# Merging two split weight loads and splitting the load of x in a one-token attention and MLP block

## The chip, the cores and the metric

The kernel runs on one core of a Trainium2 chip. The metric is the device time of one execution in microseconds (us). Most executions of this kernel agree within 0.3%. A profiled execution has a span somewhat shorter than its time: 136.3 us of 138.12 us for the kernel before. Positions below ("at 82 us") are counted from the start of the profiled span.

## The reference

One decoding step for a batch of 4. Attention with 32 query heads and 4 key/value heads over the last 2048 positions is followed by a gated MLP. Each part has a layernorm ahead of it and a residual around it. All data are bfloat16.

```python
h  = x + attention(layernorm(x), k_cache, v_cache, wq, wo)     # wq 1024x4096, wo 4096x1024
hn = layernorm(h)
h2 = h + (silu(hn @ w1) * (hn @ w3)) @ w2                      # w1, w3 1024x3584, w2 3584x1024
```

Each weight is read once: 8 MiB each of wq, K, V and wo, and 7 MiB each of w1, w3 and w2. That is 55.6 MB for four rows of activations, so the question is whether the load stream ever stops.

## The kernel before

All large loads share one ring of 160 KiB in each of the 128 partitions. The sync engine's queue issues them in a fixed plan, each as soon as the bytes that it overwrites have been read.

```python
    plan = [
        ("wq", load_rows, (0, wq_v, N_Q, 0, 4)),            # runs of 32 KiB per partition
        ("wq", load_rows, (32 * KIB, wq_v, N_Q, 4, 4)),
        ("k", load_kv, (64 * KIB, A_k_cache, 0)),
        ("k", load_kv, (96 * KIB, A_k_cache, 2)),
        ("v", load_kv, (128 * KIB, A_v_cache, 0)),
        ("v", load_kv, (0, A_v_cache, 2)),
        ("wo", load_rows, (32 * KIB, wo_v, D, 0, 32)),      # 64 KiB
        ("w1", load_rows, (96 * KIB, w1_v, N_F, 0, 8)),     # 56 KiB
        ("w3", load_rows, (0, w3_v, N_F, 0, 4)),            # 28 KiB
        ("w3", load_rows, (28 * KIB, w3_v, N_F, 4, 4)),
        ("w2", load_rows, (56 * KIB, w2_v, D, 0, 17)),
        # ... cut: three smaller pieces of w2
    ]
    # ... cut
    x_sb = act.tile([B, D], BF16)
    nc.scalar.dma_start(out=x_sb[:], in_=x_flat)
    load_next(5)
    # ... cut: layernorm of x_sb, transposed to xnT; x is loaded again, spread, as x_q
    for kc in range(KC):                                    # 8 rows of wq in each partition
        # ... cut: 8 matmuls q_ps <- xnT[kc], wq row kc
        if kc == RQ - 1:
            load_next()                                     # second half of v, over wq's first rows
    # ... cut: K transposes, scores, softmax, output product OT
    for i in range(IO):
        # ... cut: 4 matmuls y_ps <- o4, wo row i
        if i == 11:
            load_next()
    load_next()
    # ... cut: residual, second layernorm -> hnT
    gate_up("w1", g_ps)
    # ... cut: eg, gs: the silu of g_ps
    gate_up("w3", u_ps)
    nc.vector.tensor_tensor(out=hg[:], in0=u_ps[:, :, :HF], in1=gs[:], op=ALU.mult)
    # ... cut: hg transposed to hgT, then 112 matmuls y2_ps <- hgT, w2 rows
```

## Time and profile before

Before the prediction there were three runs, with a median of 138.23 us (138.06 to 138.29).

| reading | value | view |
|---|---|---|
| share of the load queue in the span of 16 DMA engines | 95.3% | page, queues |
| first and last packet of that queue | 1.74 us, 132.67 us | the trace's packet records |
| bytes over that stretch | 55.58 MB in 130.9 us, 424 GB/s | the same |
| normalised second row (hnT) ready, w1 there | 92.3 us, 99.1 us | timeline |
| hgT ready, first piece of w2 there | 122.0 us, 126.3 us | timeline |

The packet records hold the start, duration and size of every packet of every DMA queue. Grouped by size, the packets of the load queue have nearly constant durations: 84 ns for 2 KiB, 611 for 16, 1062 for 28, 1213 for 32, 2116 for 56 and 2418 for 64 KiB. A straight line through them is 8.7 ns + 0.0368 ns per byte.

First the page of the kernel before: the DMA engines' busy tenths in 40 slices of the span, the load queue (packets, MB, share of 16 engines) and the chain that ended last.

```profile
DMA  5999899999999999997988989989799999989960
...
q1 hardware_dynamic: 2592, 55.58, 95.3%
...
DMA 58%; PE 21%; ACT 13%; DVE 5%; issue 1%; SPq 0%; ACTq 0%
```

The DMA row is at 8 or 9 tenths nearly everywhere after the first slice. In its middle the chain runs through TensorE and ScalarE work, which is not a contradiction. Loads were queued ahead of that work, so the stream went on while the chain followed the computation.

Next, the waits of the kernel before: who waited, for whom, us in total, times, the longest.

```profile
PE q_ps L215 <- DMA ring<-in_A_wq_dram: 12.0, 2, 6.1
...
PE g_ps L403 <- DMA ring<-in_B_w_dram: 9.0, 1, 9.0
PE u_ps L403 <- DMA ring<-in_B_w_dram: 8.3, 2, 5.3
PE y_ps L433 <- DMA ring<-in_B_w_dram: 8.3, 3, 7.1
...
PE y_ps L353 <- DMA ring<-in_A_wo_dram: 2.0, 1, 2.0
```

TensorE waits for every weight in turn, so it has time to spare in each stage that reads a weight. The timeline of the kernel before (start, duration, engine, line, what, idle before it):

```profile
13.05 3.58 PE L215 MATMUL q_ps<-ring,xnT 128*4 128x512 bf16 x32 [6.05 <-DMA ring<-in_A_wq_dram]
...
22.55 3.15 PE L215 MATMUL q_ps<-ring,xnT 128*4 128x512 bf16 x32 [5.92 <-DMA ring<-in_A_wq_dram]
...
107.50 3.13 PE L403 MATMUL u_ps<-ring,hnT 128*32 128x448 bf16 x32 [3.00 <-DMA ring<-in_B_w_dram]
...
115.98 3.17 PE L403 MATMUL u_ps<-ring,hnT 128*32 128x448 bf16 x32 [5.34 <-DMA ring<-in_B_w_dram]
...
120.33 1.70 DVE L425 STREAM_TRANSPOSE hgT<-hg 128x896 bf16<-128x896 bf16 x1
...
126.30 3.82 PE L433 MATMUL y_ps<-ring,hgT 128*32 128x256 bf16 x68 [7.14 <-DMA ring<-in_B_w_dram]
```

Half of the q and u matmuls run while the other half of their weight is still on its way. hgT is ready 4.3 us before w2's first piece.

### The profile page before, as it was taken

The page shows a single profiled execution, that of the slowest core. Times are in us where ns is not written, and L with a number is a line of the kernel's source. Part 1 is how long each engine was busy: PE and PEld are TensorE (multiplying, and loading weights), DVE is VectorE, ACT ScalarE, POOL GpSimd, SP SyncE. Part 2 cuts the span into 40 slices and gives each one's busy share as a digit, 9 for nine tenths or more (in the row PEclk, how much of TensorE's full clock was granted, in tenths as well). Part 3 has the DMA queues.
Part 4 walks back from the last instruction along what each step waited for, and adds up shares of the span by engine and source line. Part 5 has one row for each costly group of instructions (what it writes and reads, how often), then busy time and mean ns, then how long its engine had stood idle before and what let it go on. Part 6 is the DMA issues. An engine that isn't in the chain of part 4 may idle for free.

```text
span 136.3 us, 2302 instructions
## 1 busy us (share of the span) xinstructions
PE 67.9 (50%) x1035; PEld 42.9 (31%) x1035; DVE 42.6 (31%) x73; ACT 31.0 (23%) x36; POOL 1.7 (1%) x8
## 2 busy tenths in 40 slices
PE   0101803698989889105259538830096440900960
PEld 0100201274656565001149427610043210300840
DVE  6440000244444444609940030160000695070000
ACT  0400000155555646092944000000003300000001
POOL 5000000000000000000000000000000000000000
PEclk9999999999999999965555865897557777555577
DMA  5999899999999999997988989989799999989960
GB/s 156 462 462 443 385 413 418 423 447 423 428 437 409 437 437 423 435 582 341 538 385 365 524 365 442 459 353 522 328 412 463 434 437 447 429 388 409 426 261 5
DMA packets 2662, 55.75 MB, mean 409 GB/s; under 512 B 312, under 2 KB 344, under 8 KB 604
## 3 DMA queue, kind: packets, MB, share of 16 engines
q1 hardware_dynamic: 2592, 55.58, 95.3%
q8 instruction: 8, 0.13, 0.3%
q10 hardware_dynamic: 60, 0.02, 0.1%
q14 instruction: 2, 0.02, 0.0%
HBM read 55.59 MB, written 0.01 MB: 408 GB/s over the span
## 4 chain that ended last, share of the span: by engine, by line
DMA 58%; PE 21%; ACT 13%; DVE 5%; issue 1%; SPq 0%; ACTq 0%
DMA ring<-in_B_w_dram 42%; DMA ring<-in_A_wq_dram 16%; PE kt_ps L263 9%; ACT kT L269 6%; PE scores_ps L248 5%; ACT z L304 3%; PE q_ps L215 2%; PE g_ps L403 2%; DVE rmax L280 2%; ACT Pm L285 2%; PE OT_ps L326 2%; DVE pT L294 1%; DVE z L300 1%; ACT L285 1%; DVE q_sb L225 1%
## 5 line engine op out<-in xcount | busy, mean ns | idle before, releaser
L269 ACT COPY kT<-kt_ps 128x1024 bf16<-128x1024 bf16 x16 | 15.8, 1014 | 12.0 <-PE kt_ps L263 12.0
L263 PE MATMUL kt_ps<-ident,ring 128*128 128x128 bf16 x256 | 16.4, 219 | 0.0
L263 PEld LDWEIGHTS <-ring 128*128 128x128 bf16 x256 | 14.3, 98 | 5.0 <-issue 4.9
L267 DVE COPY kT<-kt_ps 128x1024 bf16<-128x1024 bf16 x16 | 11.1, 691 | 15.2 <-PE kt_ps L263 15.2
L215 PE MATMUL q_ps<-ring,xnT 128*4 128x512 bf16 x64 | 6.7, 596 | 12.0 <-DMA ring<-in_A_wq_dram 12.0
L403 PEld LDWEIGHTS <-hnT 128*32 128x32 bf16 x128 | 5.3, 137 | 23.1 <-issue 20.5
L248 PE MATMUL scores_ps<-kT,qz 128*32 128x512 bf16 x64 | 9.9, 609 | 3.1 <-ACT kT L269 3.1
L326 PE MATMUL OT_ps<-z,ring 128*128 128x32 bf16 x256 | 7.4, 185 | 6.7 <-ACT z L304 5.0
L403 PE MATMUL u_ps<-ring,hnT 128*32 128x448 bf16 x64 | 6.3, 572 | 8.3 <-DMA ring<-in_B_w_dram 8.3
L403 PE MATMUL g_ps<-ring,hnT 128*32 128x448 bf16 x64 | 5.4, 525 | 9.0 <-DMA ring<-in_B_w_dram 9.0
L433 PE MATMUL y_ps<-ring,hgT 128*32 128x256 bf16 x112 | 5.7, 370 | 8.4 <-DMA ring<-in_B_w_dram 8.3
L326 PEld LDWEIGHTS <-ring 128*128 128x128 bf16 x256 | 7.3, 103 | 7.4 <-issue 7.4
L433 PEld LDWEIGHTS <-hgT 128*32 128x32 bf16 x112 | 4.4, 129 | 10.3 <-issue 6.1
L215 PEld LDWEIGHTS <-xnT 128*4 128x4 bf16 x64 | 2.1, 116 | 16.2 <-issue 15.9
L353 PE MATMUL y_ps<-ring,o 128*32 128x256 bf16 x128 | 5.8, 365 | 2.0 <-DMA ring<-in_A_wo_dram 2.0
L443 ACT CAST res<-y_ps 128x256 bf16<-128x256 f32 x1 | 0.4, 372 | 26.5 <-PE y_ps L433 26.5
L304 ACT ACTIVATE z<-pt_ps,mask 128x512 bf16<-128x512 f32 x8 | 5.3, 687 | 3.5 <-DVE z L300 3.5
L225 DVE TENSOR_SCALAR q_sb<-q_ps 128x512 bf16<-128x512 f32 x1 | 0.7, 690 | 17.2 <-PE q_ps L215 17.2
L353 PEld LDWEIGHTS <-o 128*32 128x32 bf16 x128 | 4.8, 130 | 3.8 <-issue 3.1
L300 DVE TENSOR_SCALAR z<-pt_ps,mask 128x512 bf16<-128x512 f32 x8 | 5.5, 740 | 1.2 <-ACT z L304 0.8
L296 PE MATMUL pt_ps<-pT,perm 128*128 128x512 bf16 x4 | 2.4, 607 | 6.8 <-DVE pT L294 6.8
L417 DVE RECIPROCAL eg<-eg 128x896 f32<-128x896 f32 x1 | 5.8, 5753 | 0.0
(73 smaller groups left out, 40.5 us busy)
## 6 DMA issues: line engine op xcount, KB each, us to landing
ring<-in_A_wq_dram SPq DMA_DIRECT2D x2, 4096.0 KB, 16.8
ring<-in_A_k_cache_dram SPq DMA_DIRECT2D x4, 2048.0 KB, 25.5
ring<-in_A_v_cache_dram SPq DMA_DIRECT2D x4, 2048.0 KB, 40.2
ring<-in_B_w_dram SPq DMA_DIRECT2D x1, 7168.0 KB
ring<-in_B_w_dram SPq DMA_DIRECT2D x2, 3584.0 KB, 28.6
ring<-in_B_w_dram SPq DMA_DIRECT2D x1, 4352.0 KB
ring<-in_B_w_dram SPq DMA_DIRECT2D x1, 1792.0 KB
ring<-in_B_w_dram SPq DMA_DIRECT2D x1, 768.0 KB
```

The lines of the kernel that those rows point to most:

```text
L215: nc.tensor.matmul(q_ps[QD * g : QD * g + B, hf * 512 : (hf + 1) * 512], lhsT=xnT[:, kc, :], rhs=wq_t[:, c0 : c0 + 512], start=(kc == 0), ...
L248: nc.tensor.matmul(scores_ps[QD * g : QD * (g + 1), n * 512 : (n + 1) * 512], lhsT=qz[:, b, g * QD : (g + 1) * QD], rhs=kT_v[:, g, :, :], ...
L263: nc.tensor.transpose(out=kt_ps[:, jj, :], in_=k_v[:, n * NJ + t * TB + jj, :], identity=ident[:])
L267: nc.vector.tensor_copy(out=kT[:, t * TB : (t + 1) * TB, :], in_=kt_ps[:])
L269: nc.scalar.copy(out=kT[:, t * TB : (t + 1) * TB, :], in_=kt_ps[:])
L300: nc.vector.tensor_scalar(out=z[:, :, g, :], in0=pt_ps[:], scalar1=mask[:, g : g + 1], scalar2=None, op0=ALU.mult)
L304: nc.scalar.mul(out=z[:, :, g, :], in_=pt_ps[:], mul=mask[:, g : g + 1])
L326: nc.tensor.matmul(OT_ps[:, b, :], lhsT=loaded["v"][b][:, j, :], rhs=PTz[j // NJ][:, (j % NJ) * B + b, :, :], start=(j == 0), stop=(j == J ...
L353: nc.tensor.matmul(y_ps[QD * j : QD * (j + 1), :], lhsT=o4[:, i, :, :].rearrange("p b s -> p (b s)"), rhs=loaded["wo"][i][:, j * CG : (j + ...
L403: nc.tensor.matmul(out_ps[QD * j : QD * (j + 1), hf, :HF], lhsT=hnT[:, k, :], rhs=loaded[kind][k][:, c0 : c0 + HF], start=(k == 0), stop=( ...
L417: nc.vector.reciprocal(out=eg[:], in_=eg[:])
L433: nc.tensor.matmul(y2_ps[QD * j : QD * (j + 1), :], lhsT=hgT[:, i, :], rhs=loaded["w2"][i][:, j * CG : (j + 1) * CG], start=False, stop=(i ...
```

## The change

The intent is larger DMA packets and fewer loads. wq becomes one load with runs of 64 KiB and w3 one load with runs of 56 KiB. w3 can then be issued only after wo's twelfth row has been read, because it lies over wo's first twelve rows. The second half of v, which lies over wq's first rows, is now issued after all q matmuls instead of after half of them. x is loaded in three column pieces. The loads share eight semaphores in turn, so the split of x also shifts which earlier load each later load's issue waits for.

```diff
-        ("wq", load_rows, (0, wq_v, N_Q, 0, 4)),
-        ("wq", load_rows, (32 * KIB, wq_v, N_Q, 4, 4)),
+        ("wq", load_rows, (0, wq_v, N_Q, 0, 8)),
 ...
-        ("w3", load_rows, (0, w3_v, N_F, 0, 4)),
-        ("w3", load_rows, (28 * KIB, w3_v, N_F, 4, 4)),
+        ("w3", load_rows, (0, w3_v, N_F, 0, 8)),
 ...
-    nc.scalar.dma_start(out=x_sb[:], in_=x_flat)
-    load_next(5)
+    for c0, c1 in ((0, 512), (512, 768), (768, D)):
+        nc.scalar.dma_start(out=x_sb[:, c0:c1], in_=x_flat[:, c0:c1])
+    load_next(4)
 ...
-        if kc == RQ - 1:
-            load_next()
+    load_next()
 ...
-        if b % BS == BS - 1:
+        if b == BS - 1:
             load_next()
```

## The prediction

> **What bounds the kernel now.** The load stream. The page's row of queues gives the weight/cache queue 95.3% of 16 engines' span and 55.58 MB of the 55.75 MB moved. The trace's packet records show that queue's 16 engines busy without a break from 1.74 us to 130.8-132.7 us of a 136.3 us span: 55.58 MB in 130.9 us, 424 GB/s. The Trainium skill, "DMA: Bandwidth & Descriptors", section "Specifications", gives a fabric ceiling of 435 GB/s; the trace agrees (a 64 KiB packet takes 2.418 us, 27.1 GB/s on one engine, 434 GB/s on 16). The chain of waits that ended last gives DMA 58%, but its middle (27 to 73 us, K transposes, softmax) is tensor work that never starved the queue: every load was issued before its predecessors drained.
>
> **What the change removes.** Packets. Durations by size fit 8.7 ns + 0.0368 ns/B (2 KiB 84 ns, 16 KiB 611, 28 KiB 1062, 32 KiB 1213, 56 KiB 2116, 64 KiB 2418). wq goes from 16 packets of 32 KiB per engine to 8 of 64 KiB, w3 from 16 of 28 KiB to 8 of 56 KiB: 16 x 8.7 ns, plus two 9 ns semaphore writes: 0.16 us less of a 131 us stream. All of it is on the critical path, because the stream is.
>
> **What it adds and moves, and the slack.**
> 1. q matmuls: half ran at 13.05-16.6 us, under wq's second half. Now all 64 wait for wq, about 22.2 us, and need 6.5 us (3.58+3.15 before), ending near 28.8 instead of 25.7. But K's first tile only landed at 27.4, where the transposes began; so attention moves later by about 2 us (eight q transposes now fall inside it).
> 2. That shift reaches w1's issue (73.2 to about 75.4 us, needed before wo drains near 80), and the wo product (start 82.2 to about 83-84; it waited 2.0 us for wo). The normalised row was ready at 92.3 and w1 landed at 99: 9.0 us of wait shrink to 7 or 8.
> 3. w3's issue waits for wo's twelfth row, near 86 us; needed by 97.
> 4. u matmuls: half ran early (107.5-110.6). Now all 64 start at about 115.8 and take 6.3 us; hg, transpose then end near 125.1 instead of 122.1. w2's first piece lands at 126.3 (7.1 us of wait, "y_ps waits for DMA"): about 1 us slack remains. This is the tightest place.
> 5. x in three pieces: two more tiny loads, alternating with wq's packets on four engines. The records show x_q's packets and semaphore writes one 32 KiB packet (1.22 us) apart; with 64 KiB packets 2.42 us. The Trainium skill, same page, "Queues, rings and completion order", says engines round-robin between queues at packet granularity; the trace agrees. The last x piece then lands at some 12-17 us instead of 2.5, and the normalised x is ready by 17-22 us: still about in time for wq at 22.2.
> 6. Semaphore rotation (eight shared): the second K load now waits for wq's landing; the first K load (4.9 us) covers its issue.
>
> **Time.** 138.23 - 0.16 = 138.05 us, range 137.6 to 138.5. Faster by over 2%: 0.01; within 2%: 0.96; slower by over 2%: 0.03.
>
> **What would show it.** Queue share and 420-odd GB/s unchanged; one wait of q_ps for wq, about 15 us or less if x is late; one wait of u_ps for w3, near 11 us; y_ps's wait for w2 down from 7.1 to 4 us in its first part or 8.3 to about 5 in total; last packet near 132.5 us.
>
> **What would make it wrong.** A gap in the queue at 26 us (second K load late) or at 80 us (w1 late); x landing after 18 us; hgT after 126.2 us because of a lower granted clock; long packets running at another rate.

## The result, and the profile after

The changed kernel took 138.33 us (median of 6 runs, 138.09 to 138.38) beside 138.19 us for the kernel before (6 runs, 138.04 to 138.40). The ratio is 1.0006, with a 95% interval of 0.9993 to 1.0019. Ratios here are the mean time of one kernel's fast runs over that of the other's of the same rounds, so they are not quite the ratio of the quoted medians. A change that touches 15 MiB of loads moved the time by less than the noise.

The page of the changed kernel:

```profile
DMA  9797796999999999998998989989899998999960
...
q1 hardware_dynamic: 2304, 55.58, 95.2%
...
DMA 56%; PE 25%; ACT 11%; DVE 4%; issue 1%; ACTq 0%; SPq 0%
```

There are 288 packets fewer, the same bytes and the same share. The load queue's last packet ended at 132.76 us, against 132.67 before. The 7s among the first slices are not pauses: by the packet records a mean of 15.99 to 16.0 engines was busy from 5.7 to 21.7 us. Packets of 2.4 us are probably too long for slices of 3.4 us to share out evenly.

The waits of the changed kernel:

```profile
DVE stats L157 <- DMA x_sb<-in_A_x_dram: 12.2, 1, 12.2
PE u_ps L401 <- DMA ring<-in_B_w_dram: 11.5, 1, 11.5
...
PE y_ps L431 <- DMA ring<-in_B_w_dram: 6.0, 3, 4.8
...
PE g_ps L401 <- DMA ring<-in_B_w_dram: 5.6, 1, 5.6
...
PE q_ps L214 <- DMA ring<-in_A_wq_dram: 4.6, 1, 4.6
```

TensorE still waits for each weight except wo, whose wait of 2.0 us is gone. The waits of g_ps (for w1) and y_ps (for w2) are shorter by 3.4 and 2.3 us: that much reserve was spent. The timeline of the changed kernel at the same places:

```profile
22.71 6.53 PE L214 MATMUL q_ps<-ring,xnT 128*4 128x512 bf16 x64 [4.63 <-DMA ring<-in_A_wq_dram]
...
116.21 5.45 PE L401 MATMUL u_ps<-ring,hnT 128*32 128x448 bf16 x64 [11.53 <-DMA ring<-in_B_w_dram]
...
122.84 1.70 DVE L423 STREAM_TRANSPOSE hgT<-hg 128x896 bf16<-128x896 bf16 x1
...
126.48 3.82 PE L431 MATMUL y_ps<-ring,hgT 128*32 128x256 bf16 x68 [4.82 <-DMA ring<-in_B_w_dram]
```

All 64 matmuls of q and of u now start with their weight's landing. hgT is ready 2.5 us later than before (124.54 us) and still 1.9 us before w2's first piece.

### The profile page after: what moved, and what is told of

Same layout as the page of the kernel before. It is cut to its first block, busy times and chain, and to the rows that moved or that the text cites. A ratio compares the mean times of both kernels' runs of the same rounds, so it can differ in the third digit from the quotient of the medians.

```text
span 136.5 us, 2303 instructions
## 1 busy us (share of the span) xinstructions
PE 67.2 (49%) x1035; PEld 42.1 (31%) x1035; DVE 42.4 (31%) x73; ACT 31.1 (23%) x36; POOL 1.7 (1%) x8
## 3 DMA queue, kind: packets, MB, share of 16 engines
q1 hardware_dynamic: 2304, 55.58, 95.2%
## 4 chain that ended last, share of the span: by engine, by line
DMA 56%; PE 25%; ACT 11%; DVE 4%; issue 1%; ACTq 0%; SPq 0%
DMA ring<-in_B_w_dram 40%; DMA ring<-in_A_wq_dram 16%; PE kt_ps L261 10%; PE scores_ps L246 6%; ACT kT L267 5%; PE q_ps L214 5%; ACT z L302 3%; PE g_ps L401 2%; DVE rmax L278 2%; ACT Pm L283 2%; PE OT_ps L324 2%; DVE pT L292 1%; DVE z L298 1%; ACT L283 1%; PE qt_ps L227 1%
## 5 line engine op out<-in xcount | busy, mean ns | idle before, releaser
L261 PE MATMUL kt_ps<-ident,ring 128*128 128x128 bf16 x256 | 17.1, 220 | 0.0
L246 PE MATMUL scores_ps<-kT,qz 128*32 128x512 bf16 x64 | 10.5, 609 | 2.6 <-ACT kT L267 2.6
L401 PE MATMUL u_ps<-ring,hnT 128*32 128x448 bf16 x64 | 5.4, 524 | 11.5 <-DMA ring<-in_B_w_dram 11.5
L171 PE MATMUL tp_ps<-ident,xn 4*128 4x4 bf16 x8 | 0.6, 199 | 17.4 <-DVE xn L164 17.4
L171 PEld LDWEIGHTS <-xn 4*128 4x128 bf16 x8 | 0.6, 160 | 17.4 <-DVE xn L164 17.4
L157 DVE BATCH_NORM_STATS2 stats<-x_sb 4x6 f32<-4x512 bf16 x2 | 1.4, 682 | 12.2 <-DMA x_sb<-in_A_x_dram 12.2
```

The source lines that it names most:

```text
L246: nc.tensor.matmul(scores_ps[QD * g : QD * (g + 1), n * 512 : (n + 1) * 512], lhsT=qz[:, b, g * QD : (g + 1) * QD], rhs=kT_v[:, g, :, :], ...
L261: nc.tensor.transpose(out=kt_ps[:, jj, :], in_=k_v[:, n * NJ + t * TB + jj, :], identity=ident[:])
L401: nc.tensor.matmul(out_ps[QD * j : QD * (j + 1), hf, :HF], lhsT=hnT[:, k, :], rhs=loaded[kind][k][:, c0 : c0 + HF], start=(k == 0), stop=( ...
```

## The experiments

The main theory, S, says that the load stream alone sets the time, and that the change saves a few packets there and spends only idle time elsewhere. One rival, C, says that the late matmuls do cost time and cancel a real gain. Another, X, says that the pieces of x disturb the start of the stream and cancel a gain. Eleven kernels ran, all correct.

### The parts one by one

Three kernels make one part of the change alone, and the fourth undoes one part.

```diff
 e1_w3_only: before, with
-        ("w3", load_rows, (0, w3_v, N_F, 0, 4)),
-        ("w3", load_rows, (28 * KIB, w3_v, N_F, 4, 4)),
+        ("w3", load_rows, (0, w3_v, N_F, 0, 8)),
 e2_x_only: before, with
-    nc.scalar.dma_start(out=x_sb[:], in_=x_flat)
+    for c0, c1 in ((0, 512), (512, 768), (768, D)):
+        nc.scalar.dma_start(out=x_sb[:, c0:c1], in_=x_flat[:, c0:c1])
 e3_wq_only: before, with
-        ("wq", load_rows, (0, wq_v, N_Q, 0, 4)),
-        ("wq", load_rows, (32 * KIB, wq_v, N_Q, 4, 4)),
+        ("wq", load_rows, (0, wq_v, N_Q, 0, 8)),
 e4_x_whole: the changed kernel, with x in one piece as before
```

> The kernel before with only w3 as one load. Theory S (the time follows the packet stream alone): eight packets fewer per engine at 8.7 ns, so the stream ends 0.08 us earlier and the ratio is 0.9994; u_ps waits once for w3, about 11 us, and w2's first wait shrinks from 7.1 to about 5 us without cost. Rival C (the late start of the u matmuls costs part of the time): ratio above 1.002, hgT after w2's first piece has landed.

> The kernel before with only x in three pieces. Theory S: no change (ratio 1.000 within 0.001); the last x piece lands near 8.5 us (two wq packets ahead of it, then one 1.21 us packet between each of its packets), before wq's first half at 13.05, so no engine that matters waits. Rival X (the x pieces disturb the stream's start and give back what the larger packets save): ratio 1.001 to 1.002 and the sum of the excess of the first 16 packets over 1.213 us above the 7.5 us seen in before.

> The kernel before with only wq as one load, x whole. Theory S with a slow start of large packets: the eight packets saved are worth 0.07 us, but the first 16 packets exceed 2.418 us by about 0.7 us each (0.47 us in before), so ratio 1.001 and stream end 0.1 to 0.2 us later. Rival X (x pieces are what slows the first packets): the excess stays at 0.47 us and the ratio is 0.9995.

> The changed kernel with x in one piece again. Theory S: x is there at 2.5 us, the normalised x at 7 us, and the time is that of the changed kernel (ratio to before 1.000 to 1.001), because x was never late for wq. Rival X: the first packets are quick again and the ratio is 0.999 or less.

| run | median us | before, same rounds | ratio, 95% interval |
|---|---|---|---|
| e1_w3_only | 138.21 | 138.18 | 0.9999 (0.9982 to 1.0015) |
| e2_x_only | 138.43 | 138.18 | 1.0015 (0.9998 to 1.0031) |
| e3_wq_only | 138.31 | 138.18 | 1.0006 (0.9989 to 1.0024) |
| e4_x_whole | 138.44 | 138.18 | 1.0012 (0.9993 to 1.0030) |

No part moves the time beyond its interval, so there is no large gain and loss that cancel. For the large version of rival X, and for the large version of rival C as far as w3 is concerned, that is the end. In e1_w3_only hgT was ready at 124.5 us, before w2's first piece at 126.4 (view of the tile hgT: shortest, median and longest duration in ns, first and last start in us):

```profile
L432 PE MATMUL y_ps<-ring,hgT x112: 269/417/421, 126.4 to 133.1; 128*32 128x256 bf16 x112
L424 DVE STREAM_TRANSPOSE hgT<-hg x1: 1700/1700/1700, 122.8 to 122.8; 128x896 bf16<-128x896 bf16 x1
```

Each expected size (0.05 to 0.2%) is below what these intervals can tell.

The pieces of x arrive late, but nobody needs them earlier. In e2_x_only the last piece's semaphore came at 9.9 us (8.5 expected). In the changed kernel it came at 15.0 us. With x whole, in e4_x_whole, the normalised x was ready near 7.3 us instead of 18.3, and the time did not improve. That matters, because e2_x_only alone would fit rival X: its ratio of 1.0015 lies where X put it. With x whole, though, e4_x_whole has a ratio of 1.0012 where X asked for 0.999 or less, and the largest loss at the start in the table below (an excess of 0.77 us). A small version of X, up to about 0.3%, is not excluded by the times.

The stream itself can be read more finely than the time. From the packet records, each engine's start on K is the moment at which wq is over on it, and its start on w2 is the end of w3. The trace does not name the engines, but each engine ends each load with a write to a semaphore, so 16 such writes give the 16 ends. Their means:

```text
wq packets   runs                                        excess of wq's    mean start
                                                         packets, us       on K, us
32 KiB       before, e1, e2, e6, e7                      0.55 to 0.69      21.94 to 22.00  (mean 21.97)
64 KiB       after, e3, e4, e8, e9                       0.58 to 0.77      21.93 to 22.06  (mean 22.00)

w3 packets   runs                            start on w1 to start on w2, us
28 KiB       before, e2, e3, e7, e10         34.13 to 34.25  (mean 34.15)
56 KiB       after, e1, e4, e8, e9           34.08 to 34.15  (mean 34.12)
```

The runs e6 to e10 are described below; they keep the packet sizes under which they stand here. "Excess" is, for one engine, the sum of what its wq packets took over the undisturbed duration of their size. Nearly all of it falls on the very first packet of each engine, and it is there in every run. Merging wq should have brought K forward by 0.08 us and brought it forward by nothing. The saving per packet is real in the formula. About half of what is missing stands in the mean excess, 0.69 us against 0.63, but the two ranges overlap, so it is not shown that larger packets start more slowly. The 0.7 us expected for the first packets of e3_wq_only was 0.57, and its stream ended at 132.68 us, as before. (The start of the kernel before loses 8.1 us over 16 packets by the kept trace, not the 7.5 of the expectation.) Merging w3 gained 0.04 of the 0.08 us expected. Both are smaller than the scatter from run to run.

### More bytes, and more packets

The next kernels press on the stream itself. e6_plus_1mib loads 1 MiB that nobody reads. The others cut wq finer: e5_wq_4k_runs by columns, e10_wq_8k_rows one row per load, and e11_wq_alt_rows by even and odd rows.

```diff
 e6_plus_1mib: before, with this in the plan after w1, issued with it
+        ("unused", load_rows, (152 * KIB, w1_v, 4096, 0, 1)),
 e5_wq_4k_runs: before, with two loads of wq, (c0, c1) = (0, 2048) and (2048, 4096)
+        nc.sync.dma_start(out=t[:, :, c0:c1], in_=src.rearrange("(p i) n -> p i n", i=KC)[:, :, c0:c1])
 e10_wq_8k_rows: before, with eight loads of wq, i = 0 to 7
+        ("wq", load_rows, (8 * i * KIB, wq_v, N_Q, i, 1)),
 e11_wq_alt_rows: before, with two loads of wq, r0 = 0 and 1
+            out=t[:, :, r0, :],
+            in_=src.rearrange("p (a two n) -> p a two n", two=2, n=n)[:, :, r0, :],
```

> The kernel before with a load of 1 MiB that nobody reads (128 packets of 8 KiB on 16 engines) put between w1 and w3. Theory S (the stream alone sets the time): 8 x 0.310 = 2.48 us more, ratio 1.018. Rival C (the compute chain shares the time): clearly less than 2.4 us, because the compute chain would hide part of it.

The time was 140.70 us beside 138.17, ratio 1.0176 (1.0160 to 1.0192). The difference of the medians is 2.53 us, and the stream ended at 135.15 us instead of 132.67, 2.48 us later. The page of e6_plus_1mib:

```profile
span 139.0 us, 2303 instructions
...
q1 hardware_dynamic: 2736, 56.62, 95.4%
```

One more MiB costs its full transfer time, as theory S says, and rival C, that the computation shares the time, falls with it for the kernel before. For the changed kernel no byte was added. There the packet records speak: its stream has no pause either, and from the last packet to the end of the span it takes 3.7 us in both kernels.

> The kernel before with wq as two loads of half the columns, so its runs are 4 KiB: 128 packets per engine for wq in place of 16. Theory S (8.7 ns per packet, all on the critical path): 112 x 8.7 ns = 0.97 us more, perhaps 0.3 us less from a quicker start with small packets: ratio 1.005 to 1.007. Both halves are needed by every q matmul, so all 64 start near 22.7 us, as in the changed kernel. Rival R (packet size does not matter to the rate, the late q matmuls do): ratio as in the changed kernel, 1.0006.

> The kernel before with wq in eight loads of one row (8 KiB packets, 64 per engine in place of 16). If 8.7 ns per packet and 9 ns per load are all that more packets cost: 48 x 8.7 + 6 x 9 ns = 0.47 us, ratio 1.003, and the excess 4.9 us of the 4 KiB column halves came from something else (their stride, or packets under some size). If small packets cost much more than that in general: ratio 1.01 or more, with mean durations of the 8 KiB packets well above 0.310 us.

> The kernel before with wq as two loads, one of the even and one of the odd rows of each partition: 8 KiB packets, 64 per engine, as in the run with eight loads of one row (ratio 1.0012), but each load skips every second 8 KiB. If packet size is what made the 4 KiB column halves cost 4.9 us, this run costs as little as the eight loads did: ratio 1.001 to 1.003. If the gaps between the packets of one load are what cost, it costs 1 us or more: ratio 1.007 to 1.03, with packets of wq well above 0.309 us or pauses between them.

| run | median us | before, same rounds | ratio, 95% interval | mean start on K, us |
|---|---|---|---|---|
| e5_wq_4k_runs | 143.20 | 138.17 | 1.0352 (1.0322 to 1.0382) | 25.87 |
| e10_wq_8k_rows | 138.45 | 138.24 | 1.0012 (0.9998 to 1.0027) | 22.08 |
| e11_wq_alt_rows | 138.75 | 138.14 | 1.0044 (1.0027 to 1.0060) | 22.59 |

My figure of 0.97 us for e5_wq_4k_runs was far off: it cost 5 us. Three causes can be read from the packet records. In both kernels whose loads skip every second run, the first wq packet started at 2.18 us instead of 1.74. In e11_wq_alt_rows, with 8 KiB packets of the usual 309 ns, that start is most of the 0.6 us that it lost. The 4 KiB packets of e5_wq_4k_runs were also slow themselves: they took 184.6 ns in the mean where most took 159, and on 128 packets that is 3.3 us per engine. With the fixed cost of 112 more packets as well, K started 3.9 us later in the mean. The third cause is that the engines were not slowed equally: the first was done with wq at 25.00 us and the last at 27.38, against 21.64 and 22.21 in the kernel before. The whole stream ended 5.35 us later (138.02 us), since its end is that of the last engine. Why the 4 KiB packets were slow is open, since no run has 4 KiB packets without the skipping.

From 8 KiB to 64 KiB per packet, without skipping, the start on K varied by 0.15 us. The 48 packets more of e10_wq_8k_rows should have cost 0.47 us. They cost 0.11 us at K. A smaller excess at the start (0.45 us, beside 0.55 to 0.69 with 32 KiB packets) explains a part of the difference and the rest is open. So packet size between 8 and 64 KiB is not a lever for this load.

### The reserve that the change spent

Two kernels compute the product hg six times over, once from the kernel before and once from the changed one.

```diff
-    nc.vector.tensor_tensor(out=hg[:], in0=u_ps[:, :, :HF], in1=gs[:], op=ALU.mult)
+    for _ in range(6):
+        nc.vector.tensor_tensor(out=hg[:], in0=u_ps[:, :, :HF], in1=gs[:], op=ALU.mult)
```

> The kernel before with the product hg computed six times over in place of once: 5 x 1.13 = 5.65 us more between the u matmuls and hgT, and nothing else. The slack by the profile is 4.2 us at w2's first piece and 1.1 us in the two later waits: theory L (the change spent a part of a reserve, which nobody noticed) says +0.3 us here, ratio 1.002.

> The changed kernel with the same five extra products. Theory L: its reserve is 1.9 us at w2's first piece and 1.2 us later, so 5.65 - 3.1 = +2.5 us over the changed kernel, ratio to before 1.019. Rival R (no reserve was spent, since both kernels end their u matmuls with w3's landing): +0.3 us as in the kernel before, ratio 1.002.

On the kernel before, the extra 5.6 us cost nothing that can be measured: 138.14 us, ratio 0.9996 (0.9973 to 1.0019). On the changed kernel the same work cost about 1 us: 139.28 us beside 138.33 without it, ratio to the kernel before 1.0076 (1.0055 to 1.0097). The timeline of the kernel before with six products:

```profile
119.29 6.72 DVE L423 TENSOR_TENSOR hg<-u_ps,gs 128x896 bf16<-128x896 f32 x6 [5.25 <-PE u_ps L403]
...
127.80 5.97 PE L434 MATMUL y_ps<-ring,hgT 128*32 128x256 bf16 x112 [8.55 <-DVE hgT L426]
```

And of the changed kernel with six products:

```profile
121.02 6.72 DVE L421 TENSOR_TENSOR hg<-u_ps,gs 128x896 bf16<-128x896 f32 x6 [7.08 <-PE u_ps L401]
...
129.53 5.05 PE L432 MATMUL y_ps<-ring,hgT 128*32 128x256 bf16 x112 [8.56 <-DVE hgT L424]
```

In both, the last matmuls wait for hgT and no longer for w2, so the stream has stopped being the limit at the very end. (The profiled run of e7_before_hg6 is the slowest of its four, 138.59 us, and its last matmul ended 0.47 us later than in the kernel before; the other three took 138.00 to 138.20 us.) They start 1.7 us later in the changed kernel. That is the reserve which the merged w3 used up unseen, and rival R, that none was spent, falls. My size, +2.5 us, was too large. The matmuls of the changed kernel, once late, ran back to back in 5.05 us, where they had taken 3.82 + 1.08 + 0.90 us with waits between. The u matmuls also took 4.98 instead of 5.45 us.

### A pause of TensorE that was not explained

In the changed kernel TensorE paused 4.03 us inside the output product, put down to "issue"; before, it paused 1.68 us. First the kernel before, then the changed one: the pause and the start of the wo product.

```profile
77.67 1.54 PE L326 MATMUL OT_ps<-z,ring 128*128 128x32 bf16 x55 [1.68 <-issue]
...
82.25 5.76 PE L353 MATMUL y_ps<-ring,o 128*32 128x256 bf16 x128 [2.04 <-DMA ring<-in_A_wo_dram]
...
82.70 1.65 PE L324 MATMUL OT_ps<-z,ring 128*128 128x32 bf16 x55 [4.03 <-issue]
...
86.16 5.57 PE L351 MATMUL y_ps<-ring,o 128*32 128x256 bf16 x128 [0.82 <-DVE o L340]
```

A packet of the instruction queue ends 1.3 to 1.5 us before the work goes on in both. One kernel loads wo with small packets, to see whether such a fetch waits behind large ones.

```diff
-        ("wo", load_rows, (32 * KIB, wo_v, D, 0, 32)),
+        ("wo", load_rows, (32 * KIB, wo_v, D, 0, 8)),     # and rows 8, 16 and 24 likewise, all
+        ...                                               # four issued where the one was
```

> The changed kernel with wo in four loads of eight rows (16 KiB packets, 32 per engine in place of 8 of 64 KiB). Theory F (PE's instruction fetch waits behind the packets queued on its engine, so its length follows their size): PE's pause inside the output product, put down to issue (4.03 us in the changed kernel, 1.68 in before), falls below 1 us, and the normalised row is ready some 3 us before the 96.0 us of the changed kernel. The time does not gain: 24 packets x 8.7 ns = 0.21 us more, ratio to before 1.002. Rival (the pause has nothing to do with packet size): it stays between 1.5 and 4 us.

The pause was 1.73 us:

```profile
79.71 1.54 PE L327 MATMUL OT_ps<-z,ring 128*128 128x32 bf16 x55 [1.73 <-issue]
```

That is what the kernel before had with 64 KiB packets, and e4_x_whole, also with 64 KiB packets, paused 1.66 us. Across the kernels with 64 KiB packets of wo the pause lay between 1.64 and 4.03 us. My theory that its length follows the packet size falls. What sets it is open. The time was 138.58 us, ratio 1.0023 (1.0006 to 1.0040), as the 0.21 us for 24 more packets per engine, and some noise, would have it.

## Why the prediction was right

The forecast was 138.05 us, within 137.6 to 138.5, and "within 2%" at 0.96. The time was 138.33 us. The reason given, that the stream sets the time and the change barely alters the stream, is what the runs show: 1 MiB more costs its full 2.5 us, while 5.6 us more of computation near the end costs nothing in the kernel before. The number alone proves little: any change that leaves the time as it was would have met the range, and the forecast gain of 0.16 us is below what these runs can tell. Point by point:

- **The stream bounds the kernel.** Right: 95.2% against 95.3% of the engines' span, and the added MiB cost 2.53 us for 2.48 expected. The Trainium skill, page "DMA: Bandwidth & Descriptors", section "Specifications", puts the fabric's ceiling at 435 GB/s. A 64 KiB packet in 2.418 us on each of 16 engines is 434 GB/s, and the whole stream ran at 424.
- **0.16 us fewer packets, all of it gained.** Mis-sized. The stream ended 0.09 us later instead of 0.16 earlier. For wq the term measured +0.03 us in place of -0.08, partly because the first packets lost more in the mean; for w3 it measured -0.04 in place of -0.08. The difference is inside the run-to-run scatter, so its sign is not settled.
- **q late, attention about 2 us later.** The q matmuls started at 22.71 us and took 6.53 (22.2 and 6.5 predicted). w1 was issued at 75.90 us (75.4 predicted; 73.22 before), so the shift was 2.7 us and not 2. The first engine was done with wo at 80.0 us, 4 us after the issue.
- **The wo product at 83 to 84 us, g's wait down to 7 or 8 us.** Wrong in size: it started at 86.16 us, and the wait for w1 fell to 5.6 us. The missing step is the longer pause of TensorE, 4.03 instead of 1.68 us, which no step of the prediction had. Reserve covered it.
- **w3's issue.** At 88.96 us (86 predicted), with w1's packets running until 96.9 us on the first engine and 98.8 on the last. Nothing waited for it.
- **hgT at 125.1 us with 1 us of reserve.** 124.54 us, and 1.9 us of reserve. The 64 u matmuls took 5.45 instead of 6.3 us. The view of windows gives a mean granted clock of 0.60 from 116 to 122 us, 0.50 before the change.
- **x at 12 to 17 us.** The last piece landed at 15.0 us, and the normalised x was ready at 18.3 us of the 17 to 22 predicted. The Trainium skill, same page, section "Queues, rings and completion order", has each engine go round its queues packet by packet. The trace agrees: the small packets of x and their semaphore writes came 1.22 us apart behind 32 KiB packets and 2.42 to 2.44 us apart behind 64 KiB ones.
- **The second K load waits for wq's landing.** Harmless, as said: the packet records show no gap.

## What to carry to other kernels

This load queue was busy from the first microsecond to the last, so merging loads of some tens of KiB per partition had next to nothing to win: work out what the packets themselves cost (here 8.7 ns each) before editing. Such a merge is still not free. It makes the first matmul wait for the last byte and spends reserve that no time shows, so look at the remaining wait for each weight after the edit as well as at the time. To learn whether a stream really is the limit, add a load of known size and see whether its whole duration appears, then add computation and see whether it vanishes.

## What the Trainium skill lacked or had wrong

- "DMA: Bandwidth & Descriptors", section "Where 436 GB/s comes from", says that for transfers from HBM to SBUF the HBM side, about 358 GB/s per core, binds. This one core drew 424 GB/s from HBM for 131 us. The sentence does not hold here, and the same section calls a measured 425 GB/s near the fabric's rate. ("Perfetto Trace Analysis", section "Roofline", does say that a single active core can draw more than that share.)
- The same page, section "Queues, rings and completion order", says that an engine drains a whole packet, typically some 9 to 17 descriptors, before it turns to another queue, and gives no time for that. Here the turns came after each single record of up to 64 KiB, and a small load paid one such turn (2.42 us) for each of its own packets and again for its semaphore: the third piece of x was there at 15.0 us.
- No page says that the first packet of each engine is slow. (The nearest is a first-byte latency, which is not said to lie inside a packet's own duration.) In 32 KiB packets its mean loss was 0.51 to 0.66 us in five runs, in 64 KiB packets 0.57 to 0.76 us in five runs.
- No page says that a load which skips every second run starts later: its first packet came at 2.18 us instead of 1.74, in two kernels. No run separates the skipping itself from the longer access pattern that it needs.
- No page gives a packet's fixed cost on this path in ns; the sizes here fit 8.7 ns. (The nearest is a floor of about 10.5 ns per packet for small loads issued from GpSimd, "DMA: Bandwidth & Descriptors", section "Measured (HBM→SBUF, 128 partitions, SWDGE, issued from GpSimd)".) Most 4 KiB packets with skipped runs took the 159 ns that fit this too, but slow ones among them raised the mean to 184.6.
